# A fused Sinkhorn attention and token-mixing kernel: mask products first, wider weight packets, a new hand order, and X of two batches turned by transposing DMA

## The chip, the cores and the metric

One core of one Trainium2 chip. The metric is the device time of one execution in microseconds (us), lower is better. The time before is the median of three runs; the profile is of one further execution.

## The reference, cut to what matters

There are 4 batches, 8 heads, 768 positions and 64 features a head; the 768 positions are 8 blocks of 96.

```python
P = sort_net                                   # (4, 8, 8, 8)
for _ in range(5):                             # Sinkhorn
    P = exp(P - max(P, -1)); P = P / sum(P, -1); P = P / sum(P, -2)
k_sorted, v_sorted = P @ blocks(k), P @ blocks(v)      # mix whole blocks of a head
attn = softmax(q_block @ k_sorted_block.T / 8)         # inside each block of 96
x = attn @ v_sorted_block                              # heads side by side: (4, 768, 512)
W_tok = (x @ w_q) @ (x @ w_k).T / 8
out = relu(W_tok @ x) @ w_out                          # float32, (4, 768, 512)
```

## The kernel before, in words

The program is a list of small units, written out by hand in the string `ORDER` (lines 17 to 50) and issued in that order; each engine runs its own units strictly in that order, and semaphores hold a unit back until its inputs are there and its PSUM banks are free. A unit reads `K13:0`: kind K, batch 1, index 3, PSUM bank 0. A capital kind is work of TensorE (PE) and names a bank; the small letter of the same kind is the copy out of that bank, with the engine that does it (`k13:D:0`; A is ACT, D is DVE, G is POOL, S is SP). All PE work goes through the helper `mm` (line 147), all plain copies through `copy` (lines 151 and 153), so lines tell little and tiles tell more. The kinds:

- `l`: loads, issued by POOL (lines 209 to 220). `lq0` is q of batch 0, cast to bf16 on the way, 768 KB as it lands; `lp` the two weights `w_q`, `w_k` into `wqk`; `lo` is `w_out` into `wo`. q, k and v have three buffers each.
- `c`, `a`: the Sinkhorn rounds on one 32x64 tile, `c` on DVE (lines 172 to 186), `a` the exponential on ACT (line 163). `a02` also makes the mask `m_p`: eight small PE products into PSUM bank 7 and a copy (lines 164 to 167). `a03` also makes `Lx`.
- `B`, `u`, `n`: the sorted weights spread over partitions (`B`, from `PbT`), copied to `PTR` (`u`), and multiplied by the mask into `M` (`n`; for batch 0 on DVE, for the others on POOL).
- `Z`: products of zeros (`fil`) that only keep PE running.
- `Q`, `q`: q turned by PE into `QT`. `K`, `k`: k times `M`, that is sorted and turned, into `KT`. V of batch 0 goes the same way (`Y`, `y`) and is turned back (`F`, `f`) into `VT`; V of the others is sorted by `V`, `v` into `Vs` and moved by six DMAs from SP (`R`, line 302) into `VT`.
- `S`, `e`: scores of ten head-blocks, exponential on ACT into `E`. `P`, `r`, `x`: `E` times `VT`, with the row sums beside, reciprocal, and the division into `X` on DVE, in five groups a batch.
- `T`, `t`: `X` turned by PE, one of four parts of 96x1024 a unit, copied to `XT`. `J`, `j`: `XT` times `wqk` into `qkT`, in two halves. `d`: half of `qkT` moved to the other partitions (`qD`), by a DMA from SP. `W`, `w`: the key half of `qkT` turned back into `wk`. `G`, `g`: `wk` times `X`, a 64x512 matrix, `Ab`. `H`, `h`: `Ab` times `qkT` and `qD`, relu, into `mixT`. `O`, `o`: `mixT` times `wo`, copied to the four slots of `ot`. `s`: stores from SP; one for two row groups, in the last batch one for each.
- `N`: a small POOL copy that waits for V's DMAs. At the end a guard looks at the reciprocals on POOL and, only for inputs out of range, runs a slow general path.

The loops run over batches like a staircase: while batch b is in S and P, batch b-1 is in T to O, and batch b+1 in Q, K, V.

Of the kernel before, what the change touches and what calls it, by code (L numbers as in the profile page):

```python
# [16 lines left out]
ORDER = """
i02:D c00:D a01:A i00:G lq0 Z019:0 Q01:0 Q00:1 c01:D a02:A c02:D a03:A i03:G c03:D a04:A c04:D
Q03:2 a05:A c05:D Z010:3 B00:3 n01:D:3 u00:A:3 lv0 Z02:4 Y01:4 n02:D:3 lk0 n03:D:3 n00:D:3 Y03:6
y01:A:4 lq1 Q02:3 y03:D:6 q01:A:0 Y00:4 y00:A:4 q00:A:1 F01:0 q03:D:2 q02:D:3 Z03:6 K02:6 f01:D:0  # L20
K03:4 Y02:2 k02:D:6 K00:0 K01:6 n11:G lv1 k03:D:4 k01:A:6 y02:D:2 Z01:4 S05:4 e05:A:4 F03:6 k00:D:0
S04:2 S02:4 F02:7 S00:0 f03:D:6 e02:A:4 Q10:6 Q11:4 F00:5 f02:D:7 e04:A:2 e00:A:0 q10:D:6 lk1 S01:2
Q12:6 q11:D:4 f00:D:5 Q13:7 lq2 P03:0 q12:D:6 e01:A:2 n10:G S06:4 e06:A:4 V12:2 q13:D:7 r03:D:0
v12:A:2 V11:6 x03:D:0 S03:4 P04:0 r04:D:0 x04:D:0 v11:A:6 e03:A:4 P00:2 V10:6 K13:0 v10:A:6 r00:D:2
n20:G K10:4 lk2 x00:D:2 k10:A:4 lp K11:2 K12:6 k13:D:0 n21:G k12:D:6 S15:0 P01:4 r01:D:4 k11:A:2
S16:2 e16:A:2 P02:6 S12:2 x01:D:4 e15:A:0 Q21:4 r02:D:6 R14:S R15:S Q20:5 e12:A:2 R13:S R10:S R12:S
x02:D:6 S10:0 S13:2 e10:A:0 q20:D:5 T00:6 T02:7 t02:D:7 e13:A:2 t00:D:6 q21:D:4 S11:0 e11:A:0 T03:5
T01:7 S14:2 e14:A:2 t03:D:5 Q23:6 K20:0 lv2 K21:4 lk3 R11:S k20:A:0 q23:D:6 K23:2 k21:D:4 Q22:6
t01:A:7 K22:0 q22:D:6 n31:G P12:4 k23:A:2 J01:7 k22:A:0 j01:A:7 r12:D:4 x12:D:4 P11:2 J00:6 S20:0
n30:G P10:4 r11:D:2 j00:A:6 S26:6 d01:S e20:A:0 x11:D:2 r10:D:4 W00:2 x10:D:4 e26:A:6 W01:3 lq3  # L30
V22:0 P13:6 w01:A:3 V21:3 w00:D:2 T11:2 r13:D:6 T10:5 v22:A:0 R25:S V20:0 x13:D:6 t10:D:5 v20:D:0
S22:6 v21:A:3 S24:3 t11:D:2 G00:5 d00:S e22:A:6 e24:A:3 G01:5 K32:6 R23:S g00:D:5 P14:0 K31:2 K33:4
k32:A:6 k31:A:2 r14:D:0 T12:6 lv3 x14:D:0 S21:0 T13:7 H02:2 e21:A:0 h02:A:2 k33:D:4 R20:S t12:D:6
H00:4 R24:S K30:0 t13:D:7 Q32:7 R22:S Q31:6 Q33:2 Q30:3 h00:D:4 k30:A:0 q33:D:2 S25:4 S23:0 R21:S
q30:D:3 q32:A:7 e23:A:0 lo q31:D:6 J11:2 J10:3 e25:A:4 S34:6 H01:0 e34:A:6 j11:D:2 V31:4 j10:D:3
P23:2 W10:6 h01:D:0 v31:A:4 r23:D:2 W11:7 w10:D:6 V32:0 w11:A:7 P22:4 x23:D:2 r22:D:4 v32:A:0 d11:S
V30:6 P21:2 v30:A:6 O02:0 O03:1 x22:D:4 P24:4 r21:D:2 P20:6 x21:D:2 o03:A:1 r24:D:4 O00:3 R31:S
T21:1 t21:A:1 G10:2 x24:D:4 o00:A:3 r20:D:6 R34:S o02:D:0 x20:D:6 G11:2 S36:4 S30:0 R30:S s01:S
S32:6 R35:S T20:3 e36:A:4 e30:A:0 O04:4 t20:D:3 g10:D:2 d10:S T22:5 e32:A:6 S33:0 o04:D:4 R33:S
R32:S t22:A:5 S31:2 H10:6 T23:4 h10:D:6 O01:5 t23:D:4 e31:A:2 e33:A:0 O05:2 H12:6 o01:A:5 H11:3  # L40
o05:A:2 h12:D:6 S35:0 s00:S J20:5 j20:A:5 J21:2 P31:6 O14:5 h11:A:3 e35:A:0 r31:D:6 s02:S x31:D:6
j21:A:2 O12:4 o12:A:4 P34:0 P32:6 O11:2 r34:D:0 d21:S O10:4 r32:D:6 o11:A:2 x32:D:6 P30:6 W21:2
o14:A:5 x34:D:0 P33:0 o10:D:4 O15:5 r30:D:6 O13:4 W20:3 w21:A:2 T31:2 x30:D:6 o15:D:5 T30:5 w20:D:3
s10:S r33:D:0 o13:A:4 G20:4 d20:S t30:A:5 x33:D:0 G21:4 T32:3 T33:0 t31:D:2 g20:A:4 H22:6 H21:4
t33:A:0 H20:1 N35:G h21:A:4 h20:A:1 t32:D:3 J30:3 J31:0 j31:A:0 O22:4 s11:S s12:S j30:D:3 d30:D
W30:5 O20:3 W31:0 O23:1 w31:A:0 o23:A:1 w30:D:5 o20:D:3 G30:5 G31:5 h22:D:6 d31:D g30:D:5 N15:G
O21:3 H30:0 N25:G o21:A:3 o22:D:4 s21:S H32:6 O24:5 h30:D:0 O25:4 h32:A:6 o24:A:5 H31:2 s20:S
o25:A:4 O31:7 s22:S h31:D:2 O35:6 O33:2 O30:3 o31:A:7 O34:7 o35:D:6 O32:6 o30:D:3 o33:A:2 s31:S
s35:S s33:S o34:A:7 s30:S s34:S o32:A:6 s32:S
"""  # L50


# [1 line left out]
def kernel(  # L54
# [100 lines left out]
    def bf(n):  # L155
        return PS[:, n, :].bitcast(BF16)
# [5 lines left out]
    def u_a(b, n, e, bank):  # L162
        nc.scalar.activation(Pv, Pv, ACT.Exp)  # L163
        if n == 2:
            for j in range(NB):
                mm(PS[:, 7, 0:SP], idb, idb[:, j * SP:(j + 1) * SP], start=(j == 0), stop=(j == NB - 1))
            nc.scalar.copy(m_p, PS[:, 7, 0:SP])
# [193 lines left out]

    def u_J(b, n, bank):
        for pt in range(PT):
            mm(PS[:, bank, 0:S // 2], wqk[:, pt].rearrange("p a d -> p (a d)"),
               XT[b % 2][:, pt, n * 384:(n + 1) * 384], start=(pt == 0), stop=(pt == PT - 1))

    def u_j(b, n, e, bank):
# [7 lines left out]
            copy(e, o, i)  # L375

    def u_W(b, n, bank):
        for ii in range(4):
            i = 4 * n + ii
            mm(bf(bank)[0:BLK, ii * P:(ii + 1) * P], qkT[b % 2][:, i * BLK:(i + 1) * BLK], idb, t=True)  # L380

    def u_w(b, n, e, bank):
        copy(e, wk[b % 2][:, 4 * n:4 * n + 4, :],
             bf(bank)[0:BLK, 0:4 * P].rearrange("p (i x) -> p i x", x=P)[:, :, DH:P])

    def u_G(b, n, bank):
# [262 lines left out]
```

## Time and profile before

| what | value |
|---|---|
| median of three runs | 109.78 us (109.6 to 109.91) |
| profiled execution | 110.02 us |
| its span, first to last instruction | 107.8 us |
| busy PE, DVE, ACT, POOL | 93.8, 74.1, 65.9, 26.5 us |
| DMA | 19.34 MB, mean 179 GB/s; 10.09 MB of it through POOL's loads |
| packets under 512 bytes | 1936 of 19359 |

Busy time of PE is from a model of pipelined matmuls, so units of PE are better measured from start to start. In the page, "idle before" is the time in which an engine stood still before an instruction, and the name behind the arrow is what ended it; "issue" stands for no cause that the profile shows. PEclk is the granted clock of PE in tenths.

### The profile page before, as it was taken

The page shows a single profiled execution, that of the slowest core. Times are in us where ns is not written, and L with a number is a line of the kernel's source. Part 1 is how long each engine was busy: PE and PEld are TensorE (multiplying, and loading weights), DVE is VectorE, ACT ScalarE, POOL GpSimd, SP SyncE. Part 2 cuts the span into 40 slices and gives each one's busy share as a digit, 9 for nine tenths or more (in the row PEclk, how much of TensorE's full clock was granted, in tenths as well). Part 3 has the DMA queues.
Part 4 walks back from the last instruction along what each step waited for, and adds up shares of the span by engine and source line. Part 5 has one row for each costly group of instructions (what it writes and reads, how often), then busy time and mean ns, then how long its engine had stood idle before and what let it go on. Part 6 is the DMA issues. An engine that isn't in the chain of part 4 may idle for free.

```text
span 107.8 us, 3505 instructions
## 1 busy us (share of the span) xinstructions
PE 93.8 (87%) x1499; PEld 64.1 (59%) x1499; DVE 74.1 (69%) x146; ACT 65.9 (61%) x95; POOL 26.5 (25%) x45
## 2 busy tenths in 40 slices
PE   5997717989998895998989599999999999999960
PEld 2335315767887784868877378676556685553420
DVE  2630765888979986696977589957756984585420
ACT  4102106527979886987878949289695269347440
POOL 7930006959920990000000000000100047000000
PEclk9999996699999999999999999999999999999999
DMA  0899999999999999999999810375270365009784
GB/s 3 89 200 204 204 203 205 115 199 203 205 206 204 231 235 225 204 204 208 205 231 250 198 29 0 104 249 166 88 299 26 146 228 234 3 3 383 298 324 163
DMA packets 19359, 19.34 MB, mean 179 GB/s; under 512 B 1936, under 2 KB 17424, under 8 KB 19344
## 3 DMA queue, kind: packets, MB, share of 16 engines
q0 software_dynamic: 14064, 10.09, 62.8%
q1 hardware_dynamic: 5280, 9.03, 24.0%
q8 instruction: 11, 0.18, 0.6%
q14 instruction: 4, 0.03, 0.1%
HBM read 20.19 MB, written 6.29 MB: 246 GB/s over the span
## 4 chain that ended last, share of the span: by engine, by line
PE 60%; DMA 12%; ACT 10%; DVE 8%; issue 5%; SPq 1%; POOL 0%; POOLq 0%; ACTq 0%
PE ps L147 60%; DMA Qn<-in_q_dram 7%; DMA qD<-qkT 5%; ACT E L321 5%; ACT Vs L151 3%; DVE KT L153 2%; DVE M L240 1%; DVE X L350 1%; ACT KT L151 1%; DVE tmp L182 1%; ACT Pm L163 1%; DVE Pm L179 1%; DVE tmp L177 1%; DVE tmp L178 1%; DVE tmp L183 1%
## 5 line engine op out<-in xcount | busy, mean ns | idle before, releaser
L321 ACT ACTIVATE E<-ps 96x960 bf16<-96x960 f32 (+1 forms) x28 | 23.7, 898 | 4.2 <-PE ps L147 2.2
L147 PE MATMUL ps<-wo,mixT 128*128 128x512 bf16 x96 | 22.9, 379 | 0.0
L350 DVE TENSOR_TENSOR X<-ps,Rall 96x896 bf16<-96x896 f32 (+1 forms) x20 | 20.0, 1004 | 0.6
L151 ACT COPY ot<-ps 128x512 f32<-128x512 f32 x16 | 9.3, 589 | 9.6 <-PE ps L147 9.5
L147 PEld LDWEIGHTS <-mixT 128*128 128x128 bf16 x96 | 8.6, 97 | 9.0 <-issue 0.6
L147 PE MATMUL ps<-fil 128*128 128x512 bf16 x35 | 11.2, 475 | 1.6 <-DVE fil L195 1.2
L240 POOL TENSOR_TENSOR M<-PTR,m_p 128x512 bf16<-128x512 bf16 x6 | 7.9, 1318 | 16.8 <-ACT PTR L151 10.9
L151 ACT CAST KT<-ps 128x768 bf16<-128x768 f32 x11 | 8.6, 808 | 5.1 <-PE ps L147 4.6
L147 PE MATMUL ps<-VT,E 96*128 96x65 bf16 x256 | 10.8, 193 | 0.0
L412 DVE TENSOR_SCALAR mixT<-ps 128x1024 bf16<-128x1024 f32 x7 | 8.6, 1224 | 3.1 <-PE ps L147 3.1
L147 PEld LDWEIGHTS <-KT 64*128 64x128 bf16 (+1 forms) x288 | 8.6, 98 | 3.5 <-issue 1.9
L147 PEld LDWEIGHTS <-E 96*128 96x128 bf16 x256 | 9.7, 97 | 1.6
L153 DVE CAST KT<-ps 128x768 bf16<-128x768 f32 x9 | 8.3, 953 | 3.0 <-PE ps L147 2.8
L147 PE MATMUL ps<-QT,KT 64*128 64x96 bf16 x256 | 9.3, 204 | 0.2 <-ACT E L321 0.2
L307 POOL COPY gate<-VT 6x1 bf16<-6x1 bf16 x3 | 0.5, 177 | 35.3 <-DMA VT<-Vs 35.2
L147 PE MATMUL ps<-M,Kn 128*64 128x128 bf16 x192 | 7.5, 221 | 1.5 <-ACT E L321 1.1
L147 PE MATMUL ps<-idb,Qn 128*64 128x128 bf16 x192 | 7.4, 226 | 1.1 <-DMA Qn<-in_q_dram 0.8
L151 ACT CAST Vs<-ps 128x1024 bf16<-128x1024 f32 x8 | 7.8, 1014 | 0.2
L147 PEld LDWEIGHTS <-Kn 128*64 128x64 bf16 x192 | 6.0, 109 | 3.0 <-issue 2.8
L147 PEld LDWEIGHTS <-fil 128*128 128x128 bf16 x35 | 3.9, 119 | 6.5 <-issue 3.6
L147 PE MATMUL ps<-XT,wqk 128*128 128x384 bf16 x32 | 6.2, 327 | 1.3 <-issue 1.3
L147 PEld LDWEIGHTS <-Qn 128*64 128x64 bf16 x192 | 6.2, 114 | 1.9 <-DMA Qn<-in_q_dram 1.3
(78 smaller groups left out, 136.5 us busy)
## 6 DMA issues: line engine op xcount, KB each, us to landing
out_dram<-ot SPq DMA_DIRECT2D x9, 512.0 KB, 3.2
Qn<-in_q_dram POOLq DMA_DIRECT2D x4, 768.0 KB, 14.4
Vn<-in_v_dram POOLq DMA_DIRECT2D x4, 768.0 KB, 13.0
Kn<-in_k_dram POOLq DMA_DIRECT2D x4, 768.0 KB, 13.2
VT<-Vs SPq DMA_DIRECT2D x18, 132.0 KB, 5.9
out_dram<-ot SPq DMA_DIRECT2D x6, 256.0 KB, 2.0
wo<-in_moe_w_out_dram POOLq DMA_DIRECT2D x1, 512.0 KB, 23.4
qD<-qkT SPq DMA_DIRECT2D x6, 48.0 KB, 2.6
```

The lines of the kernel that those rows point to most:

```text
L147: nc.tensor.matmul(o, w, x, is_transpose=t, start=start, stop=stop, skip_group_check=True)
L151: nc.scalar.copy(o, i)
L153: nc.vector.tensor_copy(o, i)
L163: nc.scalar.activation(Pv, Pv, ACT.Exp)
L177: nc.vector.reduce_sum(tmp, Pv, axis=AX.X)
L178: nc.vector.reciprocal(tmp, tmp)
L179: nc.vector.tensor_mul(Pv, Pv, rows(tmp))
L182: nc.vector.reduce_sum(tmp, (Pm if n == 1 else Pv).rearrange("p i j -> p j i"), axis=AX.X)
L240: ENG[e].tensor_tensor(out=M[b % 2][:, h0:h0 + hn], in0=src.unsqueeze(2).to_broadcast([P, hn, SP, NB]), in1=m_p.unsqueeze(1).unsqueeze(3). ...
L321: nc.scalar.activation(E[b % 2][:, n, 0:2 * w * BLK].rearrange("p (t a c) -> p a t c", a=2, c=BLK), PS[0:BLK, bank:bank + 2, 0:w * BLK].re ...
L350: nc.vector.tensor_mul(xo.rearrange("p (a t d) -> p a t d", a=2, d=D), avps(bank, w)[:, :, :, 0:D], Rall[:, b, n, :, 0:w].unsqueeze(3).to_ ...
L412: nc.vector.tensor_relu(o, i)
```

## The change

1. **Mask first.** The mask's eight products become a unit of their own, `A00:0`, in bank 0, the first work of PE; `a02:A:0` copies them. q of batch 0 is loaded ahead of `i00` (the identity), and POOL's clearing of tiles (`i03`) comes after four loads.
2. **Wider weight packets.** Each of `w_q` and `w_k` is loaded with four of its rows a partition, in one run of 1 KB, into a free half of the last `ot` slot; PE turns the pieces (`U00`), DVE copies them (`z01`), PE turns them back (`U01`) and DVE copies them into `wqk` (`z02`).
3. **Order.** The whole order is another one. The opening has 20 fillers for 35; `u00` is on DVE; the last batch's row groups 4 and 5 are computed, copied and stored in two column halves (`O34`, `O314`, `O35`, `O315`).
4. **W** turns the key half by a product with the right half of the identity instead of a transposition of both halves, into float32 of one bank for both units; for batches 0 to 2 one copy of 96x512 takes the place of two.
5. **X of batches 1 and 2** is turned by two DMAs a batch from SP (`D11`, `D10`, `D20`, `D21`), each of 96x2048 bf16 (two of the four parts); their T and t are gone. Batches 0 and 3 keep PE's turning.

```diff
+    def u_A(b, n, bank):
+        for j in range(NB):
+            mm(PS[:, bank, 0:SP], idb, idb[:, j * SP:(j + 1) * SP], start=(j == 0), stop=(j == NB - 1))
...
-                nc.gpsimd.dma_start(out=wqk[:, :, s, :], in_=w.rearrange("(t p) d -> p t d", p=P))
+                nc.gpsimd.dma_start(out=w16[:, s * DM // 2:(s + 1) * DM // 2],
+                                    in_=w.rearrange("(p u) d -> p (u d)", p=P))
...
+    def u_U(b, n, bank):
+        for t in range(PT):
+            if n:
+                mm(bf(bank)[:, t * P:(t + 1) * P], wT[:, t * P:(t + 1) * P], idb, t=True)
+                continue
+            for s in range(2):
+                x = (s * PT + t) * DH
+                mm(bf(bank)[s * DH:(s + 1) * DH, t * P:(t + 1) * P], w16[:, x:x + DH], idb, t=True)
...
+    def u_D(b, n, e, bank):
+        ENG[e].dma_start(out=XT[b % 2][:, 2 * n:2 * n + 2, :].rearrange("p k (i c) -> p (k i) c", c=BLK),
+                         in_=X[b % 2][:, 2 * n:2 * n + 2].rearrange("c k i m -> c (k i m)"), transpose=True)
...
-            mm(bf(bank)[0:BLK, ii * P:(ii + 1) * P], qkT[b % 2][:, i * BLK:(i + 1) * BLK], idb, t=True)
+            mm(PS[0:BLK, bank, i * DH:(i + 1) * DH], qkT[b % 2][:, i * BLK:(i + 1) * BLK], idb[:, DH:P])
...
+    def osplit(b, n):
+
+        r, m = n % 10, n // 10
+        return (r, slice(m * DM // 2, (m + 1) * DM // 2)) if b == B - 1 and r >= R6 - 2 else (r, slice(0, DM))
```

The order's opening, before and after:

```diff
-i02:D c00:D a01:A i00:G lq0 Z019:0 Q01:0 Q00:1 c01:D a02:A c02:D a03:A i03:G c03:D a04:A c04:D
-Q03:2 a05:A c05:D Z010:3 B00:3 n01:D:3 u00:A:3 lv0 Z02:4 Y01:4 n02:D:3 lk0 n03:D:3 n00:D:3 Y03:6
+i02:D lq0 c00:D a01:A i00:G c01:D A00:0 a02:A:0 lv0 c02:D a03:A Z07:0 Q01:0 c03:D a04:A c04:D Q00:1
+Q03:2 lk0 q00:A:1 a05:A Q02:3 c05:D Z09:1 B00:1 q02:D:3 n03:D:1 n00:D:1 u00:D:1 Z04:4 Y00:4 n01:D:1
+q03:A:2 y00:A:4 Y01:6 Y03:2 n02:D:1 y03:D:2 q01:D:0 y01:A:6 Y02:4 F01:6 y02:A:4 lv1 K01:1 k01:D:1
+K00:3 f01:A:6 K03:5 k03:D:5 i03:G K02:0 k00:A:3 n10:G n11:G S02:2 S05:4 S00:6 k02:A:0 F02:0 F03:1
```

The stretches with the transposing transfers, after:

```diff
+K23:4 t03:D:6 ... P13:2 k23:A:4 P14:4 ... P10:2 J00:0 Q21:1 Q20:6 lk3 r14:D:4 x14:D:4 j00:A:0
+Q22:0 r10:D:2 K22:4 q21:A:1 x10:D:2 R23:S q20:D:6 W00:3 W01:3 k22:A:4 S22:1 q22:D:0 K32:6 w00:D:3
+K30:4 R22:S e22:A:1 G00:3 S23:0 k32:D:6 k30:A:4 lq3 R24:S R21:S e23:A:0 G01:3 K31:6 S26:4 g00:D:3
+k31:D:6 S21:2 e26:A:4 R25:S S24:0 e21:A:2 R20:S e24:A:0 K33:4 k33:D:4 D11:S Q30:7 Q32:6 D10:S Q33:2
+Q31:3 S20:4 q32:D:6 q30:D:7 P21:0 q33:A:2 J10:2 r21:D:0 lv3 d00:S J11:7 e20:A:4 S25:4 x21:D:0 P20:0
+q31:A:3 d01:S j11:D:7 j10:A:2 r20:D:0 W10:7 d11:S e25:A:4 W11:7 V30:2 w10:A:7 V32:4 x20:D:0 d10:S
+v30:A:2 V31:6 P24:0 G10:2 G11:2 r24:D:0 x24:D:0 lo v31:A:6 H01:6 g10:D:2 h01:D:6 S36:0 H10:2
+v32:A:4 P22:4 e36:A:0 R30:S P23:0 R31:S r22:D:4 x22:D:4 O02:7 h10:A:2 S35:2 H00:4 o02:A:7 r23:D:0
+h00:A:4 O03:6 e35:A:2 O11:7 x23:D:0 R32:S o03:A:6 R35:S H02:0 R33:S S30:4 h02:D:0 D20:S S33:2
+o11:A:7 O00:6 e33:A:2 e30:A:4 o00:D:6 D21:S O01:7 S31:0 S34:2 o01:D:7 e31:A:0 S32:4 J21:6 R34:S
+J20:7 e32:A:4 j20:A:7 s00:S P34:0 P31:4 j21:D:6 r34:D:0 O10:6 x34:D:0 r31:D:4 x31:D:4 e34:A:2 W20:7
```

More of the change, by code (lines that the diff above doesn't have):

```diff
@@ L15 @@
 NMIX = 2
+SPQ = False
 ORDER = """
-i02:D c00:D a01:A i00:G lq0 Z019:0 Q01:0 Q00:1 c01:D a02:A c02:D a03:A i03:G c03:D a04:A c04:D
-Q03:2 a05:A c05:D Z010:3 B00:3 n01:D:3 u00:A:3 lv0 Z02:4 Y01:4 n02:D:3 lk0 n03:D:3 n00:D:3 Y03:6
-y01:A:4 lq1 Q02:3 y03:D:6 q01:A:0 Y00:4 y00:A:4 q00:A:1 F01:0 q03:D:2 q02:D:3 Z03:6 K02:6 f01:D:0
-K03:4 Y02:2 k02:D:6 K00:0 K01:6 n11:G lv1 k03:D:4 k01:A:6 y02:D:2 Z01:4 S05:4 e05:A:4 F03:6 k00:D:0
-S04:2 S02:4 F02:7 S00:0 f03:D:6 e02:A:4 Q10:6 Q11:4 F00:5 f02:D:7 e04:A:2 e00:A:0 q10:D:6 lk1 S01:2
@@ L23 @@
[L23 to L46, printed above, removed]
@@ L47 @@
-O21:3 H30:0 N25:G o21:A:3 o22:D:4 s21:S H32:6 O24:5 h30:D:0 O25:4 h32:A:6 o24:A:5 H31:2 s20:S
-o25:A:4 O31:7 s22:S h31:D:2 O35:6 O33:2 O30:3 o31:A:7 O34:7 o35:D:6 O32:6 o30:D:3 o33:A:2 s31:S
-s35:S s33:S o34:A:7 s30:S s34:S o32:A:6 s32:S
+i02:D lq0 c00:D a01:A i00:G c01:D A00:0 a02:A:0 lv0 c02:D a03:A Z07:0 Q01:0 c03:D a04:A c04:D Q00:1
+Q03:2 lk0 q00:A:1 a05:A Q02:3 c05:D Z09:1 B00:1 q02:D:3 n03:D:1 n00:D:1 u00:D:1 Z04:4 Y00:4 n01:D:1
+q03:A:2 y00:A:4 Y01:6 Y03:2 n02:D:1 y03:D:2 q01:D:0 y01:A:6 Y02:4 F01:6 y02:A:4 lv1 K01:1 k01:D:1
@@ new lines @@
+K00:3 f01:A:6 K03:5 k03:D:5 i03:G K02:0 k00:A:3 n10:G n11:G S02:2 S05:4 S00:6 k02:A:0 F02:0 F03:1
+f02:D:0 e02:A:2 V12:2 f03:D:1 e05:A:4 S06:4 e00:A:6 S04:0 v12:A:2 F00:6 V11:2 e04:A:0 e06:A:4
+v11:A:2 f00:D:6 S01:6 lk1 P03:0 e01:A:6 r03:D:0 x03:D:0 K13:4 V10:2 k13:D:4 K11:0 P01:6 r01:D:6
+K10:4 v10:A:2 k11:A:0 S03:2 lq1 n20:G k10:A:4 K12:0 k12:A:0 Q11:4 R15:S Q10:5 Q13:0 x01:D:6 q11:D:4
+lp Q12:1 q10:D:5 U00:4 z01:D:4 S11:6 e03:A:2 lv2 q13:A:0 P02:2 q12:D:1 e11:A:6 S12:4 r02:D:2 P04:0
+S15:6 x02:D:2 r04:D:0 lk2 R14:S n21:G e12:A:4 S13:4 e15:A:6 P00:2 R12:S U01:6 x04:D:0 S14:0 n30:G
@@ new lines @@
+r00:D:2 T01:7 e13:A:4 z02:D:6 x00:D:2 R10:S R13:S e14:A:0 t01:D:7 R11:S T02:6 t02:D:6 V21:4 P12:0
+S16:2 v21:A:4 e16:A:2 T00:7 T03:6 r12:D:0 V22:4 n31:G P11:2 x12:D:0 V20:0 t00:D:7 v22:A:4 v20:A:0
+lq2 r11:D:2 K23:4 t03:D:6 K21:6 x11:D:2 S10:0 P13:2 k23:A:4 P14:4 k21:D:6 e10:A:0 r13:D:2 K20:6
+Q23:0 J01:1 q23:A:0 x13:D:2 j01:A:1 k20:A:6 P10:2 J00:0 Q21:1 Q20:6 lk3 r14:D:4 x14:D:4 j00:A:0
+Q22:0 r10:D:2 K22:4 q21:A:1 x10:D:2 R23:S q20:D:6 W00:3 W01:3 k22:A:4 S22:1 q22:D:0 K32:6 w00:D:3
+K30:4 R22:S e22:A:1 G00:3 S23:0 k32:D:6 k30:A:4 lq3 R24:S R21:S e23:A:0 G01:3 K31:6 S26:4 g00:D:3
@@ new lines @@
+o11:A:7 O00:6 e33:A:2 e30:A:4 o00:D:6 D21:S O01:7 S31:0 S34:2 o01:D:7 e31:A:0 S32:4 J21:6 R34:S
+J20:7 e32:A:4 j20:A:7 s00:S P34:0 P31:4 j21:D:6 r34:D:0 O10:6 x34:D:0 r31:D:4 x31:D:4 e34:A:2 W20:7
+o10:A:6 P33:0 W21:7 s10:S P30:2 O05:4 s01:S w20:A:7 d20:S r33:D:0 r30:D:2 O04:7 G20:5 x33:D:0 G21:5
+x30:D:2 d21:S o05:A:4 H11:0 o04:D:7 g20:D:5 H12:2 P32:6 r32:D:6 x32:D:6 h11:A:0 T30:5 T33:4 O13:0
+h12:D:2 t30:A:5 T31:5 T32:6 t33:D:4 O12:7 o13:D:0 t32:A:6 O15:2 H21:3 H20:0 o12:A:7 H22:6 t31:D:5
+h21:A:3 O14:5 h20:A:0 J31:3 O23:4 o15:D:2 J30:0 O22:1 j31:A:3 o14:D:5 W31:5 s02:S j30:D:0 W30:0
@@ L50 @@
+O20:3 s11:S w30:A:0 O21:0 G30:2 h22:D:6 o22:A:1 o23:A:4 w31:D:5 G31:2 O24:1 d31:D g30:D:2 o21:A:0
+d30:D o24:D:1 o20:A:3 H32:6 h32:A:6 s21:S s20:S O25:0 o25:A:0 H31:4 s12:S s22:S H30:2 O314:6
+h31:A:4 h30:D:2 o314:D:6 O315:0 o315:D:0 O35:7 O32:4 o35:D:7 s314:S s315:S O30:0 s35:S o30:A:0
+O33:7 O34:0 o33:A:7 o32:D:4 O31:4 o34:D:0 s32:S o31:A:4 s30:S s33:S s34:S s31:S
 """
@@ L109 @@
     Qn, Kn, Vn = (tiles(n, NIN, [P, H, R6, D]) for n in ("Qn", "Kn", "Vn"))
-    wqk = sb.tile([P, PT, 2, DH], BF16, name="wqk")
+    wqk = sb.tile([P, PT, 2 * DH], BF16, name="wqk")
     wo = sb.tile([P, PT, DM], BF16, name="wo")
@@ L125 @@
     ot = tiles("ot", NOT, [P, 2, DM], FP32)
+    if SPQ:
+        q32 = XT[0].rearrange("p t s -> p (t s)").bitcast(FP32).rearrange("p (h r d) -> p h r d", r=R6, d=D)
+        nc.sync.dma_start(out=q32.rearrange("p h r d -> p h (r d)"),
+                          in_=q[0, 0:H // 2].rearrange("h (p r) d -> p h (r d)", p=P))
+    w16, wT = (ot[NOT - 1].rearrange("p a n -> p (a n)").bitcast(BF16)[:, n * DM:(n + 1) * DM] for n in range(2))
     M = tiles("M", 2, [P, H, SP, NB])
@@ L164, in u_a @@
         if n == 2:
-            for j in range(NB):
-                mm(PS[:, 7, 0:SP], idb, idb[:, j * SP:(j + 1) * SP], start=(j == 0), stop=(j == NB - 1))
-            nc.scalar.copy(m_p, PS[:, 7, 0:SP])
+            nc.scalar.copy(m_p, PS[:, bank, 0:SP])
         elif n == 3:
@@ L307, in u_N, with u_z @@
         nc.gpsimd.tensor_copy(gate[0:R6, :], VT[b % 2][0:R6, NB - 1, H - 1, 0:1])
+    def u_U(b, n, bank):
[6 more added lines that the diff above has]
+                mm(bf(bank)[s * DH:(s + 1) * DH, t * P:(t + 1) * P], w16[:, x:x + DH], idb, t=True)
+    def u_z(b, n, e, bank):
+        if b == 1:
+            copy(e, Qn[0][:, 2 * n:2 * n + 2], q32[:, 2 * n:2 * n + 2])
+        elif n == 1:
+            copy(e, wT.rearrange("x (p u) -> x p u", u=PT), bf(bank)[:, 0:DM].rearrange("x (u p) -> x p u", u=PT))
+        else:
+            copy(e, wqk.rearrange("p t d -> p (t d)"), bf(bank)[:, 0:DM])
     def u_S(b, n, bank):
@@ L363, in u_J @@
         for pt in range(PT):
-            mm(PS[:, bank, 0:S // 2], wqk[:, pt].rearrange("p a d -> p (a d)"),
+            mm(PS[:, bank, 0:S // 2], wqk[:, pt, :],
                XT[b % 2][:, pt, n * 384:(n + 1) * 384], start=(pt == 0), stop=(pt == PT - 1))
@@ L377, in u_W @@
     def u_W(b, n, bank):
-        for ii in range(4):
-            i = 4 * n + ii
-            mm(bf(bank)[0:BLK, ii * P:(ii + 1) * P], qkT[b % 2][:, i * BLK:(i + 1) * BLK], idb, t=True)
+        for i in range(4 * n, 4 * n + 4):
+            mm(PS[0:BLK, bank, i * DH:(i + 1) * DH], qkT[b % 2][:, i * BLK:(i + 1) * BLK], idb[:, DH:P])
     def u_w(b, n, e, bank):
-        copy(e, wk[b % 2][:, 4 * n:4 * n + 4, :],
-             bf(bank)[0:BLK, 0:4 * P].rearrange("p (i x) -> p i x", x=P)[:, :, DH:P])
+        i0, i1 = (4 * n, 4 * n + 4) if b == B - 1 else (0, NB)
+        copy(e, wk[b % 2][:, i0:i1, :].rearrange("p i x -> p (i x)"), PS[0:BLK, bank, i0 * DH:i1 * DH])
     def u_G(b, n, bank):
@@ L412, in u_h @@
             nc.vector.tensor_relu(o, i)
+    def osplit(b, n):
+        r, m = n % 10, n // 10
+        return (r, slice(m * DM // 2, (m + 1) * DM // 2)) if b == B - 1 and r >= R6 - 2 else (r, slice(0, DM))
     def u_O(b, n, bank):
+        r, c = osplit(b, n)
         for t in range(PT):
-            mm(PS[:, bank, :], mixT[b % NMIX][:, t // 2, t % 2, n, :], wo[:, t, :],
+            mm(PS[:, bank, c], mixT[b % NMIX][:, t // 2, t % 2, r, :], wo[:, t, c],
                start=(t == 0), stop=(t == PT - 1))
@@ L422, in u_o @@
     def u_o(b, n, e, bank):
-        copy(e, oslot(b, n)[:, n % 2, :], PS[:, bank, :])
+        r, c = osplit(b, n)
+        copy(e, oslot(b, r)[:, r % 2, c], PS[:, bank, c])
     def u_s(b, n, e, bank):
@@ L429, in u_s @@
         else:
-            ENG[e].dma_start(out=od[:, n, :], in_=oslot(b, n)[:, n % 2, :])
+            r, c = osplit(b, n)
+            ENG[e].dma_start(out=od[:, r, c], in_=oslot(b, r)[:, r % 2, c])
     def guard():
@@ L609 @@
         b, n = int(name[1]), int(name[2:])
-        if kind.isupper() and kind not in "RN":
+        if kind.isupper() and kind not in "RND":
             fns[kind](b, n, int(arg[0]))
```

## The prediction

> **What bounds the kernel now.** I read the page's slices first, then the chain that ended last, then the timeline of the opening, then the busy time of two long stretches. The slices are 2.695 us each.
>
> ```profile
> PE   5997717989998895998989599999999999999960
> PEclk9999996699999999999999999999999999999999
> DMA  0899999999999999999999810375270365009784
> ```
>
> TensorE (PE) is nearly full from slice 8 (21.6 us) on, and the DMA engines are full until slice 22: all inputs are loaded in one stream that ends at about 63 us. The chain, in order of time (start, length, what):
>
> ```profile
> 1.46 7.53 DMA Qn<-in_q_dram
> ...
> 10.22 0.17 ACT m_p L167
> 10.39 0.16 ACT Pm L163
> ...
> 61.62 42.61 PE ps L147 x511
> ```
>
> Two things carry it. At the end, PE works 42.6 us without a gap. At the start, the Sinkhorn rounds (ACT's exponential, then six DVE steps) stand still. The timeline says why (start, length, operation, idle before it and what ended that):
>
> ```profile
> 10.22 0.17 ACT L167 CAST m_p<-ps 128x16 bf16<-128x16 f32 x1 [5.31 <-PE ps L147]
> ...
> 15.84 0.35 PE L147 MATMUL ps<-PbT,Lx 32*128 32x32 bf16 x8 [2.94 <-DVE PbT L186]
> ...
> 17.90 0.85 PE L147 MATMUL ps<-M,Vn 128*64 128x128 bf16 x12 [0.66 <-DVE M L240]
> ```
>
> The mask copy `m_p` waits 5.31 us on ACT, because its eight matmuls stand in PE's queue behind Q01 and Q00, which wait for the first load of q. The next exponential is behind that copy. And after PE has idled 2.94 us for `PbT`, twelve matmuls take 0.85 us where 0.42 is usual (PEclk shows 6 there).
>
> ```profile
> 24.18:63.41 39.23, 34.77 (x808) 28.47 (x807) 31.69 (x53) 31.95 (x42) 11.30 (x12) 1.00 1.24 208
> 63.41:104.24 40.83, 40.81 (x492) 25.30 (x490) 28.66 (x47) 26.30 (x40) 3.76 (x10) 1.00 0.44 162
> ```
>
> Columns: length, then busy PE, weight loads, DVE, ACT, POOL, granted clock, DMA share, GB/s. The first stretch runs from the first scores (S05) to the first V product of batch 3 (V31): PE and ACT both work, neither is full. The second runs from there to PE's last matmul: PE alone sets the time. So I sum three stages.
>
> **Opening.** Rounds follow each other by 1.76 us (12.04 to 13.80, the chain's exponentials L163). With the mask's matmuls first on PE, `m_p` waits for nothing: its identity is ready at about 2.45 (now 1.31, plus the 1.14 us issue of q's load, which moves ahead of it on POOL). Rounds 3, 4 and 5 could start at 6.4, 8.2 and 9.9 instead of 10.29, 12.04 and 13.80: 3.9 us earlier. Not all of it stays. The new order puts q00 on ACT ahead of round 5. q lands at 8.98 - 0.72 = 8.26 (its issue is that much earlier). The fillers Z07 write the mask's bank and so start after `m_p`, at 5.1, seven by 0.43 us; in the trace PE ran at half pace until 5.5 us after its first matmul, so I take full pace from 10.6. Then 24 transposes at half pace (1.7 us) end at 9.97, q00 (0.80) at 10.8, round 5 and its transposition (13.80 to 15.80 now, 2.0 us) at 12.8. Z09 stands before B00: Q03 and Q02 end at 11.3, nine fillers by 0.23 (ten took 2.33) end at 13.35. B00 starts there: 2.5 earlier than 15.84. Bounds: 11.9 if all is at full pace from the start of Q, 15.6 if all is at half.
> From B00 to the first exponential of scores it is 8.8 us now (15.84 to 24.61), 3.5 us of it at half pace. New: B 0.35, two M products 0.88, Y 0.42, then ACT's y00, y01, y02, f01, k00, k02 (five by 0.75, one near Vs's 0.95) 4.7, and about 0.4 of waits: 6.75. So 20.1, **4.5 earlier; I book 4.2**, with 2.2 (half pace throughout) and 4.8 as ends. u00 moves from ACT to DVE at the same 0.37 and delays n01 only.
>
> **Middle.** From start to start a unit on PE takes: K, Q 0.42; S 0.32 (short one 0.13); P 0.44 (short 0.25); V 0.45; F 0.58; T 0.39; J 0.65; W 0.23; G 0.50; H 0.44; O 0.86. Counted by the orders, the stretch holds 22 S, 3 F, 12 Q, 10 P, 6 V, 12 K, 8 T, 4 J, 2 W, 2 G, 3 H now = 33.5, in 39.2 us. New: 21 S, 3 F, 12 Q, 12 P, 6 V, 12 K, 4 T, 4 J, 4 W, 2 G and the two U = 32.1. W moves 64 columns for 128 (between half of 0.23 and all; I take 0.18); U are 12 short transposes, 0.6 by Q's 35 ns each and rounded up. The weights' two extra copies are on DVE (0.5 each, as QT's 0.55), beside ACT. But ACT's own work grows: e 0.90 (short 0.45), v 0.95, k 0.75, q 0.75, j 0.46, h 1.0, t 0.75, w 0.36 give 33.0 now and 34.4 new (five q for one, one v more, no t, h or w). Less on one, more on the other: between -1.4 and +1.4, **I take 0**.
>
> **Late.** From V30 on: 40.4 us of PE work for 41.8 (no T of batch 2, 1.56; cheaper W; two O split in halves; the cut lies elsewhere). The stretch runs at 40.83/41.8 of the ledger, so **-1.4**. The tail (copy, issue, landing) stays.
>
> **The transposing transfers.** Four of 96x2048 bf16, 393 KB each, on SP's queue; the trace has no such operation. Nearest rows (us from issue to landing last):
>
> ```profile
> out_dram<-ot SPq DMA_DIRECT2D x9, 512.0 KB, 3.2
> ...
> VT<-Vs SPq DMA_DIRECT2D x18, 132.0 KB, 5.9
> ```
>
> By the output row a pair takes 3.2 us and 1.0 for the second (393 KB at 383 GB/s, the best slice): 4.2. By the VT row, of which six carry as much: 4.7 for issuing six (31.82 to 36.5) and 5.9 for the last = 10.6. Batch 2: D20 can issue after x22, D21 after x23; J21 and J20 need both. From P22's end to J21, PE has P23, O02, S35, H00, O03, O11, H02, S30, S33, O00, O01, S31, S34, S32 = 7.5 us; less r and x (1.3 a group), D20 has 6.2 and D21 4.9. The stall is 0 to 4.4. No input loads run there, as at the outputs, but five VT transfers are ahead of it: **+1.0**. R34 is queued behind D21 and all P of batch 3 need it: it comes due just as late. Batch 1: 9.6 us of PE units from P10 to J10, less 1.3, at the middle's pace 9.7 us; stall 0 to 0.9, **taken 0**; qD's d00 and d01 wait behind D10 on SP and have some 7 us.
>
> The Trainium skill has two rules here that disagree. "VectorE: DVE Perf Modes", section "The three transpose paths", gives 1309 ns for a 128x128 block by DMA against 390 ns on TensorE; sixteen blocks one after another would be an estimated 20.9 us per transfer, and the time that of the fourth rival below. "Advanced Engine Details and Errata", section "X-Bar Transpose (TRN2)", says that these transfers are as fast as plain ones: the forecast. No run shown so far has one, though TensorE's 49 ns per block here (eight in 0.39) is far from the first page's 390.
>
> **Input stream.** Last landings now, from issue and longest landing: q by 53.7, v by 59.1, `wo` 62.9; they are first used at 58.0, 63.4 and 66.6: about 4 us to spare, which the opening uses up. The stream gains 0.7 at its start, 0.9 from the hole at 18 to 21 us (140 GB/s for 204; v of batch 1 is now issued before POOL's M products) and something from the weights' packets (256 for 1024). Batch 1's D adds 0.79 MB, 3.9 us at 204 GB/s, at worst wholly ahead of v. Wait for v 0 to 2.1, **+0.4**.
>
> **Sum.** -4.2 + 0 - 1.4 + 1.0 + 0.4 = -4.2 against the profiled execution, 110.02 (span 107.8 and 2.2 around it): 105.8. The median, 109.78, is 0.24 below that execution; I give 105.7.
>
> **Rivals.**
> 1. *The clock stays slow in the opening.* For it: only seven fillers before q lands, and PE idle before them. Against: once running, it has work without a long gap. B00 at 15.6, gain 2.2 only: 107.7. The Trainium skill, "TensorE: Matmul & The Clock Gate", section "Part 4: PE-mode transpose", says that transposes don't count as busy for the clock, so Q would not warm it; now, 36 transposes right behind fillers ran at full pace, which neither proves nor refutes it.
> 2. *D costs what VT costs:* stalls of 4.4 and 0.9 instead of 1.0: 110.0, no change.
> 3. *All goes well:* no stall, opening 4.8, ACT no limit: 102.4.
> 4. *D goes piece by piece, and the kernel is slower.* Each D writes 16 x 128 rows of 192 bytes. A load packet takes 77 ns of one engine (62.8% of 107.8 us by 16 engines over 14064 packets); 2048 at that price over 16 engines are 9.9 us, a pair 19.7. J21 then waits some 14 us, J10 some 10: 128.7. It decides from a pair of about 10 us on, when J21's wait eats the 4.2 gained. For it: pieces far smaller than any big transfer's here. Against: VT's small pieces run beside a full stream in 5.9.
>
> **Chances.** Forecast 0.45; clock 0.13; VT-like 0.17 (0.04 faster, 0.03 same, 0.10 slower); all well 0.08; piecewise 0.17. Less than 0.3% can't be told from no change for this kernel. Faster 0.70, same 0.03, slower 0.27. The range takes in the forecast's bounds, the opening's best (102.4) and VT-like stalls with a late v (110.0 + 2.1): 102.4 to 112.5; what lies above is the fourth rival.
>
> **What would show it.** `m_p` right behind its exponential at 4.9; `PbT` done by 12.8; B00 at 13.35; the first E near 20; PE from V30 to its end in 39.5 plus J21's wait; waits of PE for DMA XT<-X; landings of XT<-X near 3 to 4 us. I am wrong if XT<-X takes over 8 us to land, or if B00 is still near 15.8.

## The result, and the profile after

The changed kernel takes **119.23 us** (117.63 to 120.99, four runs) against 109.83 for the kernel before on the same chip: the ratio is 1.076, 95% interval 1.070 to 1.083. The profiled execution took 119.84 us, with a span of 117.9. It is slower by about 9 us, where 4 us faster was forecast. The ratio is taken from undisturbed runs alone (118.62 and 117.63 us of the changed kernel), as every ratio here is, while the medians take in all runs.

The page's slices of the kernel after, now 2.95 us each, show the place:

```profile
PE   0489998867589873998360079999969999999960
PEclk9999999999999999599998555999999999999999
DMA  0999999999999999999999900076962644029783
```

Slices are counted from 0. There are dents at 8 to 10 and at 15, and a hole at 19 to 22, with two empty slices (61.9 to 67.8 us); behind the last two the granted clock is down to 5. The DMA engines are full through slice 22, 67.8 us; before they were full through slice 21 of shorter ones, 59.3 us, and busy to eight tenths in slice 22.

The chain that ended last names what PE waited for (start, length, what):

```profile
1.27 7.42 DMA Qn<-in_q_dram
...
16.97 8.46 DMA Kn<-in_k_dram
...
30.66 15.51 DMA Qn<-in_q_dram
46.16 0.04 issue
46.21 3.92 PE ps L154 x35
50.12 18.44 DMA XT<-X
...
81.03 5.32 DMA XT<-X
```

Before, the chain had one load in it, the first. Now it has three, and two transposing transfers. The transfer issued at 50.12 (`D10`, the second of batch 1's two) lands 18.44 us later; one of batch 2 takes 5.32. The waits of PE from the first exponential of scores (19.38) to the first V product of batch 3 (73.19), with the total, the number and the longest:

```profile
PE ps L154 <- DMA XT<-X: 7.7, 1, 7.7
PE ps L154 <- DMA Qn<-in_q_dram: 6.4, 3, 2.7
PE ps L154 <- DMA Kn<-in_k_dram: 1.2, 2, 0.8
```

They sum to 15.3 us. The longest stands in the profile of e3 below as well, with 7.6 us. This stretch took 38.80 before (24.61 to 63.41). PE's longest waits in it were not for loads ("issue" stands for no cause that the profile shows):

```profile
PE ps L147 <- issue: 2.1, 3, 1.3
PE ps L147 <- ACT E L321: 1.3, 2, 1.1
```

The stretch takes 53.81 now, 15.0 more: 12.3 us of it are idle time of PE (16.8 for 4.5) and 2.7 busy time (37.04 for 34.34). So the account is: opening -5.2 (first exponential at 19.38 for 24.61), middle +15.0, late stretch 0.0 (73.19 to 114.03 is 40.84, before 40.83), tail and the time outside the span 0: +9.8, as 119.84 less 110.02 is.

A wait costs more than its own length. Timeline of PE behind the hole, and the stage of the hole in two stretches (length, busy PE, weight loads, DVE, ACT, POOL, granted clock, DMA share, GB/s):

```profile
68.61 2.74 PE L154 MATMUL ps<-XT,wqk 128*128 128x384 bf16 x8 [7.70 <-DMA XT<-X]
...
86.39 1.14 PE L154 MATMUL ps<-XT,wqk 128*128 128x384 bf16 x6 [0.91 <-DMA XT<-X]
```

```profile
60.90:68.61 7.71, 0.01 (x2) 0.01 (x1) 1.33 (x2) 1.27 (x2) 0.00 (x0) 0.70 1.15 142
68.61:75.00 6.39, 6.39 (x64) 4.61 (x65) 1.88 (x3) 2.71 (x4) 0.00 (x0) 0.56 0.07 18
```

Eight products of `XT` with `wqk` take 2.74 us where 1.47 is usual, since the clock granted in the 6.39 us behind the wait is 0.56. In the 4.58 us of it that belong to the middle it is 0.50, an estimated 2.3 of the 2.7 us of more busy time. And the first of the two stretches shows whom PE waits for: DMA engines that are fully busy at only 142 GB/s. In slices 3 to 5 of the page the same engines, just as full, move 204 to 205 GB/s. They work on something costly for its bytes.

The opening came as forecast: the mask's copy stands right behind an exponential at 4.82, with no wait of its own.

```profile
4.82 0.15 ACT L172 CAST m_p<-ps 128x16 bf16<-128x16 f32 x1
...
12.80 0.36 PE L154 MATMUL ps<-PbT,Lx 32*128 32x32 bf16 x8
```

### The profile page after: what moved, and what is told of

Same layout as the page of the kernel before. It is cut to its first block, busy times and chain, and to the rows that moved or that the text cites. A ratio compares the mean times of both kernels' runs of the same rounds, so it can differ in the third digit from the quotient of the medians.

```text
span 117.9 us, 3404 instructions
## 1 busy us (share of the span) xinstructions
PE 89.6 (76%) x1433; PEld 61.1 (52%) x1440; DVE 67.9 (58%) x138; ACT 69.7 (59%) x96; POOL 25.5 (22%) x42
## 2 busy tenths in 40 slices
DMA packets 25152, 20.92 MB, mean 177 GB/s; under 512 B 7216, under 2 KB 23472, under 8 KB 25136
## 4 chain that ended last, share of the span: by engine, by line
DMA 47%; PE 42%; POOL 4%; issue 2%; DVE 1%; ACT 1%; POOLq 0%; DVEq 0%
PE ps L154 42%; DMA XT<-X 20%; DMA Qn<-in_q_dram 19%; DMA Kn<-in_k_dram 7%; POOL M L250 4%; ACT QT L158 1%; DVE M L250 1%; ACT ot L158 0%; DVE Ab L428 0%; DVE PTR L160 0%; POOLq L250 0%; DVEq L428 0%; POOLq L675 0%; POOLq L200 0%
## 5 line engine op out<-in xcount | busy, mean ns | idle before, releaser
L154 PE MATMUL ps<-wo,mixT 128*128 128x512 bf16 (+1 forms) x98 | 22.6, 362 | 0.3
L154 PE MATMUL ps<-XT,wqk 128*128 128x384 bf16 x32 | 8.7, 417 | 8.6 <-DMA XT<-X 8.6
L482 POOL CROSS_LANE_REDUCE s<-Rall 96x1 f32<-96x280 f32 x1 | 0.8, 757 | 59.5 <-DVE Rall L374 59.5
L158 ACT COPY ot<-ps 128x512 f32<-128x512 f32 x14 | 7.9, 589 | 5.3 <-PE ps L154 4.9
L158 ACT COPY QT<-ps 128x768 bf16<-128x768 bf16 x7 | 5.6, 796 | 9.1 <-PE ps L154 9.1
L158 ACT CAST Vs<-ps 128x1024 bf16<-128x1024 f32 x9 | 8.9, 1024 | 1.8 <-PE ps L154 1.8
L374 DVE RECIPROCAL Rall<-ps 96x14 f32<-96x14 f32 (+1 forms) x20 | 4.6, 230 | 9.3 <-PE ps L154 8.7
L160 DVE COPY ot<-ps 128x512 f32<-128x512 f32 (+2 forms) x13 | 7.7, 605 | 3.3 <-PE ps L154 3.1
L154 PEld LDWEIGHTS <-wqk 128*128 128x128 bf16 x32 | 3.4, 115 | 11.8 <-DMA XT<-X 7.8
L442 ACT ACTIVATE mixT<-ps 128x1024 bf16<-128x1024 f32 x7 | 7.1, 1025 | 3.4 <-PE ps L154 3.4
```

The costliest lines, as they stand in the source:

```text
L154: nc.tensor.matmul(o, w, x, is_transpose=t, start=start, stop=stop, skip_group_check=True)
L158: nc.scalar.copy(o, i)
L160: nc.vector.tensor_copy(o, i)
L374: nc.vector.reciprocal(Rall[:, b, n, :, 0:w], avps(bank, w)[:, :, :, D])
L442: nc.scalar.activation(o, i, ACT.Relu)
L482: g.tensor_reduce(s1[:, 1:2], rv, axis=AX.XYZWC, op=ALU.max)
```

## The experiments

The theory after the result: **(T1)** batch 1's transposing transfers run while the inputs are still being loaded, and there they take three times as long and more. **(T2, rival)** it is the transposing itself that is slow. **(T3, rival)** it is the input stream: a kernel that is 5 us ahead finds its inputs missing, whatever turns X. **(T4, rival)** it is the place in SP's queue: other transfers behind the transposing ones come late.

### No transposing transfer (e1)

X of batches 1 and 2 turned by PE again; the rest of the change stays. The eight T units were put where a bank is free.

```diff
- K33:4 k33:D:4 D11:S Q30:7 Q32:6 D10:S Q33:2
+ t11:D:7 e24:A:0 K33:4 k33:D:4 Q30:7 Q32:6 Q33:2
- D20:S S33:2 ... D21:S O01:7
+ S33:2 ... T22:1 t22:D:1 ... T23:0 ... t23:D:0 ... T20:6 ... t20:D:6 ... T21:7 ... t21:A:7
```

> The changed kernel with X of batches 1 and 2 turned by TensorE again (eight T, eight copies t), all else kept. Theory 'shared engines' (batch 1's transposing transfers and the input loads slow each other down): both waits go, PE's 8.6 us for XT and most of its 6.4 us for q, and the slow clock behind them; 104 to 107 us. Rival 'stream' (the new order uses inputs before they can land, with or without these transfers): the waits for q stay, 108 to 111 us. Rival 'own price' (a transposing transfer is slow by itself): as 'shared engines' here.

113.87 us, ratio 1.033 (1.023 to 1.042), above all that was expected. PE waits 2.3 for q, 1.6 for k, 1.2 for `KT` and 0.7 for `ot`. So the transfers are about half of the loss, but not all of it: without them the change is still slower than the kernel before, in spite of an opening that is 3.9 us earlier (first exponential at 20.72). Part of the rest is batch 2's T units, which I put in a stage that PE sets: from V30 to its last product PE takes 42.37 us here, and 39.29 in e2 below, where transfers turn batch 2.

### Only batch 2's transfers (e2), only batch 1's (e3)

```diff
e2: - D11:S ... D10:S     + T12:2 ... T13:2 ... T10:6 ... T11:7
e3: - D20:S ... D21:S     + T22:1 ... T23:0 ... T20:6 ... T21:7
```

> The changed kernel with batch 1 turned by TensorE, batch 2 by transposing transfers, when no load is in flight. 'Shared engines': within 1 us of the kernel without any such transfer (1.6 us of PE saved, some 0.9 us of wait added). 'Own price': 2 us or more slower than that kernel. 'Stream': as the kernel without them.

> The changed kernel with batch 1 turned by transposing transfers, batch 2 by TensorE. 'Shared engines': nearly the whole loss is here, 116 to 120 us. 'Own price': the loss is halved, 110 to 114 us. 'Stream': the wait for XT of 7.7 us stays, and the waits for q as well, 116 to 120 us.

e2: **109.5 us**, ratio 0.988 (0.977 to 1.000). e3: **121.51 us**, ratio 1.107 (1.097 to 1.116). The two pairs are the same size and the same instructions. Batch 1's alone brings the whole loss, batch 2's none. Landing times of the tile `XT` in e3, batch 1's pair (shortest, median, longest):

```profile
DMA to landing us min/median/max: 14.4/16.4/18.5
```

and in e2, from the list of DMA issues (count, median us to landing), batch 2's pair:

```profile
XT<-X SPq DMA_TRANSPOSE x2, 3.8
```

With batch 1's pair gone, some 9 us come back, more than the 7.7 of the wait; the slow clock behind the wait is one candidate for the rest. But e2 only draws level with the kernel before: in its profiled execution PE waits 3.3 for q and 2.6 for k, and in e1's 2.3 and 1.6, so T3 has a share.

### The changed kernel without batch 3's input loads (e8)

Same transfers, same queue, but three loads fewer (`lk3`, `lq3`, `lv3` left out).

```diff
- P10:2 J00:0 Q21:1 Q20:6 lk3 ... g00:D:3 ... lq3 ... r21:D:0 lv3
+ P10:2 J00:0 Q21:1 Q20:6 ... r21:D:0
```

> The changed kernel without the loads of k, q and v of batch 3 (that batch is computed from batch 0's); batch 1's transposing transfers then meet hardly any load. 'Shared engines': they land in 4 to 6 us instead of 14.4 and 18.4, PE's wait for XT is under 1.5 us, 98 to 103 us. If 14 us and more are the price of batch 1's transfers in themselves: PE still waits 5 us or more for XT, 106 us or more.

106.36 us, ratio 0.959 (0.949 to 0.969), slower than the 98 to 103 expected. Batch 1's pair, issued at 44.68 and 49.99 for 45.08 and 50.12, lands in 6.7 and 3.9 us:

```profile
DMA to landing us min/median/max: 3.9/5.3/6.7
```

PE waits 0.5 for `XT`. The first of the two still ran beside the last load, `wo`, which landed at 49.87; the second met no load. In the kernel after, `wo` landed at 68.29 and `D10` at 68.56, so that one had loads beside it for nearly all of its time. The transfer is long only beside loads: for T1, and against a price of transposing that is the same everywhere. (Leaving the loads out also takes away waits for them, so the 106.36 is not the price of the transfers alone.)

### Plain pieces (e12) and plain rows (e13) in place of batch 1's pair

Batch 1's two transfers become plain copies of 288 KB each, as the profile counts: in e12 of 1536 pieces of 192 bytes, in e13 of 96 rows of 3 KB. Neither turns X, and both clear the 32 partitions of `XT` that the copies leave out, by POOL in the opening.

```diff
+        if b == 1:
+            ENG[e].dma_start(out=XT[b % 2][0:BLK, 2 * n:2 * n + 2, :].rearrange("p k (i c) -> p (k i) c", c=BLK),
+                             in_=X[b % 2][:, 2 * n:2 * n + 2].rearrange("c k i m -> c (k i) m")[:, :, 0:BLK])
+            return
```

```diff
+            ENG[e].dma_start(out=XT[b % 2][0:BLK].rearrange("p k s -> p (k s)")[:, 1536 * n:1536 * n + 1536],
+                             in_=X[b % 2][:, 2 * n:2 * n + 2].rearrange("c k i m -> c (k i m)")[:, 0:1536])
```

> The changed kernel in which batch 1's two transfers don't transpose: each is a plain copy of 1536 pieces of 192 bytes (295 KB) from X to XT on the same queue, at the same place; 32 partitions of XT are zeros, so batch 1 is not the reference's. If small pieces beside the loads are what is slow, they land after 10 us or more and the time is 114 to 119 us. If the transposing is: they land in 4 to 7 us and the time is 108 to 112 us.

> As the run with plain pieces, but each transfer copies one row of 3 KB a partition (the same 295 KB in 96 rows); batch 1 is not the reference's. If the number of pieces decides beside the loads: it lands in 3 to 6 us, 108 to 112 us. If any transfer beside the loads is slow: as long as with pieces, 114 us or more.

e12: **116.94 us**, ratio 1.059 (1.049 to 1.069), PE waits 7.4 for `XT`. e13: **108.32 us**, ratio 0.981 (0.972 to 0.991), PE waits 0.7. The DMA issues of e12, then of e13 (count, KB each, median us to landing), and the packets of the two kernels:

```profile
XT<-X SPq DMA_DIRECT2D x2, 288.0 KB, 14.9
...
DMA packets 25120, 20.72 MB, mean 179 GB/s; under 512 B 7184, under 2 KB 23440, under 8 KB 25104
```

```profile
XT<-X SPq DMA_DIRECT2D x2, 288.0 KB, 7.1
...
DMA packets 22240, 20.72 MB, mean 195 GB/s; under 512 B 4112, under 2 KB 20368, under 8 KB 22224
```

The same bytes at the same place in the same queue: 1440 packets more in each transfer cost 7.8 us of its landing, and 8.6 us of the whole. (The rows' 7.1 is a little more than the 3 to 6 expected.) Transposing adds little to that: the transposing pair lands in 14.4 and 18.4 with 384 KB and 1568 packets each (25152 less e2's 22016, halved), 251 bytes a packet. T2 falls; T1 becomes sharper: **many small packets beside a full stream of loads**.

The Trainium skill's "Advanced Engine Details and Errata", section "X-Bar Transpose (TRN2)", says that transposing DMAs are as fast as plain ones; 14.9 by pieces against 16.4 agrees, for pieces of that size. Its "DMA: Bandwidth & Descriptors", section "Why small descriptors are slow (HBM only)", says that transfers from SBUF to SBUF don't suffer from small pieces; beside this stream they do, 14.9 for 7.1, and the measurement decides.

### The mask's products first, in the old order (e4)

The kernel before, with only the mask's eight products as a unit of their own ahead of the fillers, in their old bank.

```diff
-i00:G lq0 Z019:0 Q01:0 Q00:1
+i00:G lq0 A00:7 Z019:0 Q01:0 Q00:1
```

> The kernel before with one edit: the mask's eight products are issued as the first work of PE. PbT should be ready at about 11.9 us and B00 run at about 13 us instead of 15.84, without the slow clock behind it. If engines bind, 105.5 to 107 us. If the input stream binds behind the opening, at least half of that is given back: 108 to 109.5 us.

**106.23 us**, ratio 0.967 (0.960 to 0.974): the best kernel here, faster than both. The first exponential is at 20.02 (4.6 earlier), and PE ends at 99.78 for 104.24 (4.5 earlier). PE now waits for loads behind the opening too (1.7 of q's 2.7 lie in the opening):

```profile
PE ps L147 <- DMA Qn<-in_q_dram: 2.7, 2, 1.7
PE ps L147 <- DMA Kn<-in_k_dram: 1.6, 2, 1.4
```

In the middle, between the first exponential and the dense stretch, PE waits 2.8 us for loads and 1.7 for all else; before it was 0 and 4.3, for engines or for no cause that the profile shows. So there the loads took the place of waits that the old order had anyway, and little was lost. The granted clock in the profiled execution stays 1.00.

### Batch 2's transfers in the old order (e5, e7, e9)

e5 is the kernel before with `D21 D20` for T of batch 2, issued ahead of two VT transfers and of `d10`; e7 adds e4's edit; e9 is e7 with the pair behind `d10`.

```diff
-r20:D:6 R34:S o02:D:0 x20:D:6
+r20:D:6 R34:S o02:D:0 x20:D:6 D21:S D20:S
e9: - x20:D:6 D21:S D20:S ... d10:S      + x20:D:6 ... d10:S D21:S D20:S
```

> The kernel before with one edit: X of batch 2 is turned by two transposing transfers, issued when x20 is done, while no load is in flight. In the changed kernel with batch 1 on TensorE such a transfer landed in 3.8 us. 'Shared engines': 1 to 1.6 us faster than before (1.56 us of PE gone from the late stretch, where PE alone sets the time). 'Own price': no faster than before.

> The kernel before with two edits: the mask's products first (106.2 us alone) and X of batch 2 turned by transposing transfers. If the two add up: 104.6 to 105.3 us. 'Own price', or a stream that takes the second gain back: 106 us or more.

> The kernel before with the mask's products first and X of batch 2 turned by transposing transfers, now behind the transfer d10 in SP's queue instead of ahead of it. Theory 'queue place': the 6.9 us that the same two edits lost with the transfers ahead of d10 (qD landed 4.5 us later, PE waited 3.9 us, then ran at a slow clock) go, and the 1.56 us of PE work come back as 0.5 to 1.5 us: 104.7 to 105.8 us. Rival (transposing beside VT and qD costs in itself): 108 us or more.

e5: 116.64 us, ratio 1.055 (1.047 to 1.063). e7: 113.08, ratio 1.015 (1.005 to 1.024). e9: **106.96**, ratio 0.966 (0.955 to 0.977). e5 and e7 come out as slow as their rival 'own price' has it, but not for its reason: in all three the pair lands in 3.7 to 4.0 us. e9 lies between its two expectations. What makes e5 slow is what stands behind the pair on SP. Its SP queue (start, time to issue) and PE's wait:

```profile
70.52 3.12 SPq L356 DMA_TRANSPOSE XT<-X  x2
...
75.76 0.80 SPq L377 DMA_DIRECT2D qD<-qkT  x1
```

```profile
78.74 0.37 PE L147 MATMUL ps<-qD,Ab 64*128 64x256 bf16 x1 [4.16 <-DMA qD<-qkT]
...
79.25 3.59 PE L147 MATMUL ps<-wo,mixT 128*128 128x512 bf16 x8
```

Issuing the pair holds SP for 3.12 us, `qD` goes out at 75.76, PE stands 4.16 us, and O behind it goes at half pace (3.59 for eight products, 1.90 in the kernel after; granted clock 0.54 from 78.74 to 84.00). e9 takes back what e7 had lost to e4 by its place alone (ratios 0.966 for 1.015). So T4 is real, but in the old order with my placement; in the changed kernel batch 2's pair costs a wait of 0.9. And e9 is no faster than e4, by ratios that agree: the four T units that the pair replaces (1.56 us of PE) brought nothing that could be measured. From V30 on PE waits 1.8 us in e9 for `qD`, `VT` and `XT`, and not at all in e4. In the new order the same exchange shortens that stretch by 3.1 us (e1 against e2): what the pair is worth depends on the order around it.

### Two tries at the opening's lost gain (e6, e11)

e6 is e2 without `lk3` and `lq3` (batch 3 then uses batch 0's k and q). e11 is e2 with fillers ahead of two points where PE waited for loads.

```diff
e6:  - lk3 ... lq3
e11: - Q23:0 J01:1 ... K32:6        + Z012:7 Q23:0 J01:1 ... Z010:7 K32:6
```

> The changed kernel with batch 1 turned by TensorE (batch 2 by transposing transfers), and without the loads of k and q of batch 3: batch 3 is computed from the k and q that lie in those buffers, those of batch 0; 1.5 MB less in the input stream. 'Stream': PE's waits for q and k (5.9 us in the kernel with all loads) and the slow clock behind them go, v of batch 3 lands near 52 us instead of 60, 100 to 104 us. If the new order is bound by its engines: not below 107 us.

> The changed kernel with batch 1 turned by TensorE, and fillers ahead of the two waits for loads: twelve before Q23, ten before K32 (2.6 and 2.2 us at full pace). Theory 'clock' (a wait of some 3 us is paid a second time, as a slow clock behind it): the waits stay, the clock stays full, 106.5 to 108.5 us for 109.5 and a smaller spread between runs. If the waits alone count: 109.5 to 112 us.

e6: 108.54 us (105.62 to 109.58), too spread for a ratio, and slower than 'stream' expected. The wait for k goes to 0.2, but q's is 4.7: q of batch 2 is ahead of the loads taken out, and it still comes late, at 47.1. e11: 110.31, ratio 0.999 (0.993 to 1.005); the clock is 0.996 and the waits for q and k fall to 2.1, as the fillers stand in them, and nothing is gained. That the slow clock is the main loss of e2 has fallen. What is left are the missing inputs; that rests on the waits, and no run shows it by itself.

The landings say why. The ninth load of q, k and v lands at 45.4 before and 46.2 after (issue plus landing); the last of them at 59.1 before, 65.3 after, and 60.0 in e2. The stream's end did not move forward with the opening. Before, each input of batches 2 and 3 had 3.6 to 4.3 us to spare (q of batch 2: landed at 33.9, used at 37.48; v of batch 3: 59.1 and 63.41). An opening that is 5.2 us earlier uses that up and waits.

A second cause lies beside it, which no run takes apart from the first: the new order also puts v ahead of q in the stream. q of batch 1 lands at 30.8 for 20.5 before, q of batch 2 at 46.2 for 33.9; v of batch 2 lands at 37.2 for 45.4. e4 has almost the same opening with the old order of loads, and waits 2.8 us for loads in the middle where the changed kernel waits 7.8.

## Why the prediction was wrong, step by step

- **Opening, booked -4.2: right.** -5.2 measured, 0.4 beyond its end of 4.8. `m_p` at 4.82 (4.9 forecast), B00 at 12.80 (13.35), first exponential at 19.38 (20.1). The first rival, a slow clock here, did not come.
- **Middle 0: not refuted, and not seen apart.** The excess of 15.0 is idle time for 12.3, and most of the other 2.7 is the slow clock; the 1.4 either way of the forecast can't be seen in that.
- **Late -1.4: right, where it can be seen.** PE takes 39.29 us for this stretch in e2, 1.5 less than the 40.83 before; 39.5 was forecast. In the changed kernel it is 40.84, 0.0 where -1.4 and batch 2's +1.0 made -0.4: its first 1.8 us ran at a clock of 0.72, behind batch 1's stall.
- **Batch 2's transfers, +1.0: right** (0.91), by landings of 5.3 and 5.4 between the two rows taken as bounds.
- **Batch 1's transfers, "stall 0 to 0.9, taken 0": the step that failed.** 7.7 us, and behind it a clock of 0.56. The room was not too small: 9.7 us were forecast from the first issue to J10, and PE came there after 15.8 (45.08 to 60.90). The landing was mis-sized. The ceiling was the VT row: 5.9 us beside the full stream, six of them. Six of those carry as much, and I took bytes for the price. But a VT transfer moves rows of 1056 bytes (line 302: 132 KB in 128 rows), so its pieces are not small, as the fourth rival's "against" has it. The whole queue, VT's 18 transfers and all stores in it, had 5280 packets before for 9.03 MB, 1.7 KB each; this pair has 3136 of 251 bytes, and e12 against e13 shows that beside a stream the packets are the price. The text said that 0.79 MB take 3.9 us of the stream: the transfers took 14.4 and 18.4, and PE waited for the longer.
- **Input stream, "+0.4, at worst 2.1": failed too.** 7.6 us of waits for q and k in the middle. I compared the last landings with their first uses and found "about 4 us to spare, which the opening uses up", then priced only a late v. But q and k in the middle of the stream had no more to spare than the last ones, and they came late first. The landings were also those of the old order of loads, in which q of batch 2 lands 12.3 us earlier than in the new one. Without batch 1's transfers (e1, e2) the stream ends at 60.3 and 60.0, no earlier than before, so the 0.7 and 0.9 gained at its start did not last; with them it ends at 65.3, which is 5.3 later and not 3.9.
- **The fourth rival** (0.17) had the mechanism, small pieces, and priced a pair at 19.7 us: batch 1's took 23.5 from the first issue (45.08) to the last landing (68.56). It put the decision at J21, where no loads run and 0.9 was lost. Its 128.7 is 9.5 too high: the second stall, 14 there, was 0.9, and the waits for loads, which it did not have, fill part of that place. Its price per packet came from the load stream, and it comes near only beside that stream; alone, 1568 packets took 3.8 us.
- The estimate of 20.9 us for sixteen blocks one after another, which the prediction took from the Trainium skill's "VectorE: DVE Perf Modes", section "The three transpose paths", does not agree with 3.8 alone; the 14.4 to 18.4 beside loads come near it, but e12's plain pieces do that too.
- The range's upper end, 112.5, is more than its own sum gives (110.0 + 2.1 = 112.1); the measured time lies above both.

What stays open: how the 9 us between the changed kernel and e2 split between the wait, the clock and the loads pushed back; how the waits for q and k split between the earlier opening and the new order of loads; and what the wide weights, W by a product and the split last row groups are worth by themselves, which no run took apart.

## What to carry to other kernels

Price a transfer by its packets, and not by its bytes, where it runs beside a full stream, and don't carry over a landing seen without loads; the same instruction took 3.8 us in one place and 18.4 in the other. Before an opening is moved forward, list for each load its landing and its first use: a gain beyond the smallest gap becomes a wait there, unless the stream moves too; in e4 that wait took the place of others, and the gain stayed. Try the smallest edit by itself in the old order: the mask's products alone gave 3.3%, and what the change put around them lost it.

## What the runs showed of the hardware

- One transposing transfer of 96x2048 bf16 lands in 3.7 to 5.4 us without loads and in 14.4 to 18.5 beside them (6.7 in e8, where the loads ended on the way); issuing it held SP for 1.4 to 2.3 us without loads and in e8, and for 3.80 and 8.72 beside them in the kernel after, and the next issue on SP (`qD`) went out at 58.94, where it did at 49.81 behind e13's rows.
- After PE stood still for 7.7 us, the granted clock was 0.56 for the next 6.4; after 4.16 us, 0.54 for 5.3 (e5). The lost pace comes on top of the wait.
